# Order of decode steps and late operand loads in a float32 kernel built from seven-product blocks

## The chip, the cores and the metric

The kernel runs on one core of one Trainium2 chip. The metric is the device time of one execution in microseconds (us); before the change its median over 3 runs is 820.87 us (819.47 to 821.22). Details come from one profiled execution, which took 818.6 us itself.

## The reference

A decayed attention recurrence feeds two chains of matrix products. The weights are given as 64-bit numbers and are used as float32.

```python
y[:, :, t] = scale * einsum('bhd,bhde->bhe', q[:, :, t], state)   # 4 x 8 heads, 768 steps, 64 wide
x = y as 3072 x 512
# gated stage, d_ff 1024
a = x @ w1;  b = x @ w2
x = ((a * b) @ w3) @ w_out
# three-matrix stage, d_ff 768
h = maximum(maximum(x @ w1, x @ w2), x @ w3)
out = h @ w_out
```

## The kernel before

The stages follow one another: attention (to about 81 us), the gated stage (L577 to L579, 81.8 to 310.2 us), a merge of `w3` and `w_out` (L665), the product with the merged matrix (L750), the three-matrix stage (L876 to L878, 468.0 to 726.2 us) and the last product (L947).

Every large product is cut into blocks of seven smaller products of sums of quarters, as in Strassen's method. Numbers are split in a high and a low part, so that each piece is three matmuls. In the three-matrix stage there are 3 column groups j, 3 row blocks n in each, and 7 products q in each block: 63 products, numbered s = 7 * (3 * j + n) + q. One product is 3 parts p (one for each weight matrix) of 6 matmuls into one PSUM bank each; two sets of three banks take turns. The gated stage has 2 groups of 3 blocks of 7 products, with 4 parts of 6 matmuls.

After each part the bank is emptied: q = 0 by a ScalarE copy from bank to bank (L881, "seed": set b is then added to by q = 1; in block 0 it goes to SBUF), q = 2 and 3 by ScalarE copies (L883, L885), q = 1 and 6 by a ScalarE copy for part 0 (L891) and a VectorE maximum for the others (L889), q = 4 and 5 by VectorE (L895, then L897). The next product on the same banks can't begin before that.

Beside the products two things are prepared.

*Weights.* A 64-bit weight tile is fetched by a DMA of 512 KB (L93; it is called by a step on the ACT queue, when `late` is set, else on SP) into one of three staging tiles `stg0` to `stg2`, and decoded in steps: ScalarE L124, GpSimd L126, VectorE L147 and L149, ScalarE L156, VectorE L141 (or L135). `decode_a` issues L141 of the tile before, then L124, L147 and L149; `decode_b` issues L156, perhaps the L124 of the next tile, and the next fetch. `Spread` gives the steps out: `Spread(jobs, slots)` releases at its t-th `tick()` so many jobs that after `slots` ticks all are out. The tick stands behind each part.

*Operands.* `make_op` makes an operand by a ScalarE cast (L254) and VectorE subtractions (L255, L266 to L277) in j = 0 and stores it in DRAM; from j = 1 on `op_load` (L724) fetches it back, 1 MB each, on the ACT queue (on SP for the first ones). The buffers form a ring: 4 in j = 0 and j = 2, 6 in j = 1. The load for the next user of a buffer is issued after the last part of the product that frees it (L905 to L907).

Every engine runs its instructions in the order in which they are written, and the DMAs of ScalarE's queue stand in the order of its instructions as well: an instruction that waits holds all that stand behind it.

The lines of the change:

```python
if g or q or not n:                                           # L602
    side.tick()
side = Spread([idle] * 3 + [step] * 36, 4 * (7 * NB - LAG))   # L628
side = Spread([idle] * 2 + [step] * (4 * GH), 2 * 21 + 3)     # L831
t = heir[s]                                                   # L905
if t is not None and not len(GEN) <= t < J1:
    op_load(t)
side.tick()                                                   # L910
```

Of the kernel before, what the change touches and what calls it, by code (L numbers as in the profile page):

```python
# [26 lines left out]
NB = NT // (2 * N)  # L27
# [6 lines left out]
GH = 3  # L34
# [13 lines left out]
def fused_kernel(ctx: ExitStack, tc: tile.TileContext, ck, w12, w3t, wo1, w123, wo2, mask, gout, gch, kdec, out):  # L48
# [16 lines left out]
    def spill(n, q):  # L65
        return opsp[n, q].rearrange("h p x -> p h x")

    def halves(t):
        return t.bitcast(F32).rearrange("p (h x) -> p h x", h=2)
# [349 lines left out]
    def sets_b(blk):  # L419
        s = [bank[0:4], bank[4:8]]  # L420
        return {"a": s[blk % 2], "b": s[1 - blk % 2]}

    with tc.manual_schedule():
# [122 lines left out]
        LAG = 4  # L546
# [6 lines left out]
        side = Spread([idle] * 5 + [step] * (4 * GA), 4 * (12 + LAG))  # L553
        wgen = weights(raw_quads(1024), 1024)
        for g in range(KF // GA):
            for n in range(NB):
                blk = g * NB + n
                sets = sets_b(blk)
                for q in range(7):
                    s = 7 * blk + q  # L560
                    if g == 0:
                        if PB[q] < 0:
                            make_op(s, quad_b, 0)
                        for job in late_w.pop(s, ()):
                            job()
                    t = s + 3
                    if 7 * NB <= t < 14 * NB:
                        nc.scalar.dma_start(out=halves(op_t[t % 4]), in_=spill(t // 7 - NB, t % 7))
                    which, first = ORDER[q]
                    x = op_slot(s)  # L570
                    w = wslot(q).rearrange("p h (i k n) -> p h i k n", i=GA, k=2)
                    seeded = blk in SEED and q == 1
                    for p in range(GA):
                        ps = sets[which][p]
                        for k in range(2):
                            wh, wl = w[:, 0, p, k, :], w[:, 1, p, k, :]
                            nc.tensor.matmul(ps, wh, x[:, 0, k, :], start=first and k == 0 and not seeded, stop=False, skip_group_check=True)  # L577
                            nc.tensor.matmul(ps, wh, x[:, 1, k, :], start=False, stop=False, skip_group_check=True)  # L578
                            nc.tensor.matmul(ps, wl, x[:, 0, k, :], start=False, stop=k == 1, skip_group_check=True)  # L579
                        u, c, e = (part(nm, p) for nm in "UCE")  # L580
                        if q == 0:
                            nc.scalar.copy(out=sets["b"][p] if blk in SEED else u, in_=ps)
                        elif seeded:
                            nc.scalar.copy(out=u, in_=ps)
                        elif q == 1:
                            nc.vector.tensor_tensor(out=u, in0=u, in1=ps, op=ALU.add)
                        elif q == 2:
                            nc.scalar.copy(out=c, in_=ps)
                        elif q == 3:
                            nc.scalar.copy(out=e, in_=ps)  # L590
                        elif q == 4:
                            nc.vector.tensor_tensor(out=e, in0=ps, in1=e, op=ALU.subtract)
                        elif q == 5:
                            nc.vector.tensor_tensor(out=c, in0=c, in1=ps, op=ALU.subtract)
                            nc.vector.tensor_tensor(out=c, in0=c, in1=u, op=ALU.mult)
                            if p % 2:
                                store(fsp[n, p // 2, g], work["C"][:, p // 2 * 1024:][:, :1024], 1)
                        else:
                            nc.vector.tensor_tensor(out=e, in0=e, in1=ps, op=ALU.mult)
                            if p == GA - 1:  # L600
                                store(fsp[n, 6, g], work["E"][:, 1024:], 0)
                        if g or q or not n:  # L602
                            side.tick()
                        if g == 0 and p == PB[q]:
                            make_op(s, quad_b, 0)
                        z = p if blk > NB else 2 * q + p // 2
                        if blk and (q == 0 if blk > NB else q < 2 and p % 2):
                            fsums((blk - 1) % NB, (blk - 1) // NB, z)
                    stores()
                    z = s - 7 * (NB - 1) - LAG  # L610
                    if z == 0:
                        side.rest()
                        drain()
                    if 0 <= z < 7:
                        wgen((0, 4, 1, 2, 3, 5, 6)[z])
                    if z == 6:
                        x_st.close()
                        m_st, m_pl = stage_pool("m")
                        wo1_sb = [m_pl.tile([P, 2, 512], F32R, name=f"wo1_{k}") for k in range(KF)]
                        r_st, r_pl = stage_pool("r", "right")  # L620
                        w3_sb = [(m_pl if k > 1 else r_pl).tile([P, 2, 512], F32R, name=f"w3_{k}") for k in range(10)]
                        w3_sb += [op_t[(k // 2 + 2) % 4][:, :].rearrange("p (u h n) -> p u h n", u=2, h=2)[:, k % 2] for k in range(6)]
                        wq += [lambda k=k: fetch(wo1[k], None, wo1_sb[k][:, 0], wo1_sb[k][:, 1]) for k in range(KF)]
                        wq += [lambda k=k: fetch(w3t[k // 2, k % 2], None, w3_sb[k][:, 0], w3_sb[k][:, 1])
                               for k in range(2 * KF)]
                        wq[-7:-7] = [idle, lambda: ring.__delitem__(slice(3, 5))]
                        more(5)
                        side = Spread([idle] * 3 + [step] * 36, 4 * (7 * NB - LAG))  # L628
        side.rest()

        fraw = [work[nm][:, z * 1024:(z + 1) * 1024] for nm in "UCE" for z in range(2)]
# [42 lines left out]
        side = Spread([step] * 12, 8 * ZD)  # L674
# [42 lines left out]
        J1, J2 = 7 * NB, 14 * NB  # L717
        home_h = [z % 4 for z in range(J1)] + [(4, 5, 1, 2, 3, 0)[z % 6] for z in range(J1)] + [(2, 3, 0, 1)[z % 4] for z in range(J1)]
        bufs_h = [x[:, :] for x in op_t]
        heir = {s: next((t for t in range(s + 1, 7 * NB * GH) if home_h[t] == z), None) for s, z in enumerate(home_h)}  # L720

        def op_load(t):
            eng = nc.sync if t < J1 + 4 else nc.scalar
            eng.dma_start(out=halves(bufs_h[home_h[t]]), in_=spill(t // 7 % NB, t % 7))  # L724
# [3 lines left out]
        side = Spread([idle] * 4 + [step] * (4 * GH), 26)  # L728
        wgen = weights(raw_quads(256 * GH), 256 * GH)
        GEN = (15, 18, 21, 24, 27, 30, 33, 36)  # L730
        XL = 0
        for s in range(XS):
            n, r = divmod(s, 14)
            q, kk = divmod(r, 2)
# [90 lines left out]
        for j in range(GH):  # L825
# [2 lines left out]
                xb_st.close()  # L828
            if j + 1 < GH:
                wq += [lambda w=w, u=u: fetch_w123(j + 1, w, u) for w in range(GH) for u in range(2)]  # L830
                side = Spread([idle] * 2 + [step] * (4 * GH), 2 * 21 + 3)  # L831
            else:
                o_st, o_pl = stage_pool("o")
                wo = [o_pl.tile([P, 2, 768], F32R, name=f"wo{q}") for q in range(7)]
                raw = wraw_t[0][:, :].rearrange("p (m u k n) -> p m u k n", m=2, u=2, k=3)
                wq += [lambda k=k: fetch(wo2[k], raw[:, :, k // 3, k % 3, :]) for k in range(KH)]
                wogen = weights(raw_quads(768), 768, lambda q, n: wo[q])
                side = Spread([idle] * 2 + [step] * (2 * KH) + [drain]
                              + [lambda q=q: wogen(q) for q in (0, 1, 5, 2, 3, 4, 6)], 2 * 21 + 6)
            wgen = weights(raw_quads(256 * GH), 256 * GH)  # L840
            for n in range(NB):
                blk = j * NB + n
                sets = {"a": hbank[blk % 2], "b": hbank[1 - blk % 2]}
                m11, m21, m12, m22 = m_t[blk % 2]
                for q in range(7):
                    s = 7 * blk + q
# [25 lines left out]
                    for p in range(GH):  # L872
# [25 lines left out]
                        if p == GH - 1:  # L898
                            if s == 12:
                                xc_st.close()  # L900
                                xc_st, xc_pl = stage_pool("x2o")
                                bufs_h += [xc_pl.tile([P, 2048], F32R, name=f"opx{z}")[:, :] for z in range(2)]
                            if s in (12, 13):
                                op_load(J1 + s - 12)
                            t = heir[s]  # L905
                            if t is not None and not len(GEN) <= t < J1:
                                op_load(t)  # L907
                        if p == PH[q]:
                            make_op(s, quad_h, len(GEN))
                        side.tick()  # L910
                    if q == 1:
                        store(hsp[n, 0, :, j, :], m11)
                    elif q == 4:
# [18 lines left out]
        for s in range(7 * NB):  # L932
            n, q = divmod(s, 7)
# [99 lines left out]
```

## Time and profile before

| | |
|---|---|
| median of 3 runs | 820.87 us (819.47 to 821.22) |
| profiled execution | 818.6 us, span 816.6 us |
| PE busy | 805.8 us, 99% of the span |
| DVE busy | 631.9 us, 77% |
| ACT busy | 389.1 us, 48% |
| POOL busy | 76.0 us, 9% |
| DMA | 246.56 MB, 302 GB/s |
| granted TensorE clock | 1.00 in the gated and the three-matrix stage |

PE is TensorE's matmuls, PEld its weight loads, one ahead of each matmul; DVE is VectorE, ACT ScalarE (ACTq its queue, where it issues DMAs), POOL GpSimd, SP SyncE. A row of a timeline gives the start, the time it took, engine, line, operation, tiles, and in brackets the idle time ahead of it and who ended that. "DMA to landing" is the time from a DMA's issue to the arrival of its data.

### The profile page before, as it was taken

Reading aid. Unit: us, or ns where it says so; the run is one execution under the profiler, and the core shown is the slowest. Engines: PE = TensorE matmul, PEld = TensorE weight load, DVE = VectorE, ACT = ScalarE, POOL = GpSimd, SP = SyncE. Lnnn points to the kernel's source line nnn. Section 1 sums busy time; section 2 is a strip of 40 time slices with the busy share of each in tenths; the row PEclk is TensorE's granted clock in tenths of the full one; section 3 lists DMA queues with packets and bytes.
Section 4 is the critical chain, followed back from the end, with each engine's and each line's share of the span. In section 5 each row is a group of like instructions: output and inputs, shape, how many; then the busy total and the mean of one; then the engine's idle time right before and its main releaser. Section 6 shows DMA issues by size and latency. Waiting matters only on the chain. (4 is left out here: it accounts for less than half of the span.)

```text
span 816.6 us, 12214 instructions
## 1 busy us (share of the span) xinstructions
PE 805.8 (99%) x4648; PEld 672.5 (82%) x4648; DVE 631.9 (77%) x795; ACT 389.1 (48%) x589; POOL 76.0 (9%) x93
## 2 busy tenths in 40 slices
PE   8999999999999999999999999999999999999997
PEld 8889888888888888888888888888888888888886
DVE  3799899989698978679799848993665555588782
ACT  2432646463345454567577545453334334444642
POOL 2443000000011111001010001000000010000000
PEclk9999999999999999999999999999999999999999
DMA  9998698799999975686789798989998699956522
GB/s 346 407 407 309 226 365 344 274 342 330 388 334 417 352 307 182 241 298 212 269 301 350 275 347 306 369 292 417 394 318 306 239 335 351 326 210 215 193 104 78
DMA packets 70154, 246.56 MB, mean 302 GB/s; under 512 B 6608, under 2 KB 6736, under 8 KB 70096
## 3 DMA queue, kind: packets, MB, share of 16 engines
q1 hardware_dynamic: 48864, 165.97, 53.8%
q10 hardware_dynamic: 21232, 79.81, 27.4%
q8 instruction: 37, 0.61, 0.3%
q14 instruction: 21, 0.17, 0.1%
HBM read 163.97 MB, written 81.79 MB: 301 GB/s over the span
## 5 line engine op out<-in xcount | busy, mean ns | idle before, releaser
L577 PE MATMUL bank<-op,w 128*128 128x512 f32 x336 | 130.8, 389 | 0.0
L579 PE MATMUL bank<-op,w 128*128 128x512 f32 x336 | 130.7, 389 | 0.0
L578 PE MATMUL bank<-op,w 128*128 128x512 f32 x336 | 130.7, 389 | 0.0
L876 PE MATMUL bank<-op,w 128*128 128x512 f32 x330 | 128.6, 390 | 0.1
L878 PE MATMUL bank<-op,w 128*128 128x512 f32 x330 | 128.4, 389 | 0.0
L877 PE MATMUL bank<-op,w 128*128 128x512 f32 x330 | 128.4, 389 | 0.0
L126 POOL TENSOR_SCALAR dec<-dec 128x512 f32<-128x512 f32 x64 | 48.5, 757 | 552.8 <-ACT dec L124 516.1
L577 PEld LDWEIGHTS bank<-op,w 128*128 128x128 f32 x336 | 63.1, 188 | 13.3 <-issue 0.2
L578 PEld LDWEIGHTS bank<-op,w 128*128 128x128 f32 x336 | 63.1, 188 | 13.2
L579 PEld LDWEIGHTS bank<-op,w 128*128 128x128 f32 x336 | 63.1, 188 | 12.9
L876 PEld LDWEIGHTS bank<-op,w 128*128 128x128 f32 x330 | 61.9, 188 | 13.9 <-ACT bank L881 0.9
L878 PEld LDWEIGHTS bank<-op,w 128*128 128x128 f32 x330 | 61.9, 188 | 12.8
L877 PEld LDWEIGHTS bank<-op,w 128*128 128x128 f32 x330 | 61.9, 188 | 12.8
L752 PE MATMUL bank<-op,w 128*128 128x512 f32 x168 | 65.4, 389 | 0.0
L750 PE MATMUL bank<-op,w 128*128 128x512 f32 x168 | 65.4, 389 | 0.0
L751 PE MATMUL bank<-op,w 128*128 128x512 f32 x168 | 65.4, 389 | 0.0
L156 ACT ACTIVATE dec<-stg 128x512 int32<-128x512 uint32 x49 | 33.1, 676 | 52.4 <-DVE stg L149 46.0
L147 DVE TENSOR_SCALAR dec<-dec 128x512 int32<-128x512 int32 x64 | 27.0, 421 | 21.8 <-POOL dec L126 21.8
L124 ACT ACTIVATE dec<-stg 128x512 f32<-128x512 f32 x49 | 32.6, 665 | 13.2 <-DMA stg<-in_w_dram 7.4
L889 DVE TENSOR_TENSOR m<-m,bank 128x512 f32<-128x512 f32 x34 | 23.3, 684 | 19.6 <-PE bank L878 19.0
L948 PE MATMUL bank<-w,wo 128*128 128x512 f32 x96 | 37.4, 390 | 0.0
L947 PE MATMUL bank<-w,wo 128*128 128x512 f32 x96 | 37.4, 389 | 0.0
(216 smaller groups left out, 1581.8 us busy)
## 6 DMA issues: line engine op xcount, KB each, us to landing
op<-opsp ACTq DMA_DIRECT2D x53, 1024.0 KB, 8.1
opsp<-op SPq DMA_DIRECT2D x34, 1024.0 KB, 5.6
ck<-in_ck_dram SPq DMA_DIRECT2D x34, 512.0 KB, 10.0
fsp<-C SPq DMA_DIRECT2D x24, 512.0 KB, 4.8
op<-opsp SPq DMA_DIRECT2D x10, 1024.0 KB, 6.0
hsp<-m SPq DMA_DIRECT2D x32, 256.0 KB, 6.3
stg<-in_w_dram SPq DMA_DIRECT2D x15, 512.0 KB, 9.4
U<-fsp SPq DMA_DIRECT2D x14, 512.0 KB, 5.9
```

Of the source, the lines that this page charges most:

```text
L126: nc.gpsimd.tensor_scalar(out=df, in0=df, scalar1=MAX_HI, scalar2=MIN_HI, op0=ALU.min, op1=ALU.max)
L577: nc.tensor.matmul(ps, wh, x[:, 0, k, :], start=first and k == 0 and not seeded, stop=False, skip_group_check=True)
L578: nc.tensor.matmul(ps, wh, x[:, 1, k, :], start=False, stop=False, skip_group_check=True)
L579: nc.tensor.matmul(ps, wl, x[:, 0, k, :], start=False, stop=k == 1, skip_group_check=True)
L750: nc.tensor.matmul(ps, wh, x[:, 0, k, :], start=first and kk == 0 and k == 0, stop=False, skip_group_check=True)
L751: nc.tensor.matmul(ps, wh, x[:, 1, k, :], start=False, stop=False, skip_group_check=True)
L752: nc.tensor.matmul(ps, wl, x[:, 0, k, :], start=False, stop=kk == 1 and k == 1, skip_group_check=True)
L876: nc.tensor.matmul(ps, wh, x[:, 0, k, :], start=first and k == 0 and not seeded, stop=False, skip_group_check=True)
L877: nc.tensor.matmul(ps, wh, x[:, 1, k, :], start=False, stop=False, skip_group_check=True)
L878: nc.tensor.matmul(ps, wl, x[:, 0, k, :], start=False, stop=k == 1, skip_group_check=True)
L947: nc.tensor.matmul(ps, wh[:, k, o], xh[:, k], start=first and k == 0, stop=False, skip_group_check=True)
L948: nc.tensor.matmul(ps, wh[:, k, o], xl[:, k], start=False, stop=False, skip_group_check=True)
```

## The change

It moves no work between engines and adds or removes no instruction. Three things differ:

1. Gated stage: behind the parts of a block's first product (q = 0) a tick now comes in block 0 of each group only. Before, the second group's blocks had it too. The Spread has 60 slots in place of 68.
2. Three-matrix stage: in the first product of blocks 1 to 8 there is no tick, so no decode step. The Spreads have 39, 36 and 39 slots in place of 45, 45 and 48.
3. Three-matrix stage: the load that belongs to a block's last product (q = 6) is issued after the last seed copy of the next block's first product, together with that product's own load.

```diff
-                        if g or q or not n:
+                        if q or blk in (0, NB):
                             side.tick()
-                        side = Spread([idle] * 3 + [step] * 36, 4 * (7 * NB - LAG))
+                        side = Spread([idle] * 3 + [step] * 36, 60)
-                side = Spread([idle] * 2 + [step] * (4 * GH), 2 * 21 + 3)
+                side = Spread([idle] * 2 + [step] * (4 * GH), (39, 36)[j])
-                              + [lambda q=q: wogen(q) for q in (0, 1, 5, 2, 3, 4, 6)], 2 * 21 + 6)
+                              + [lambda q=q: wogen(q) for q in (0, 1, 5, 2, 3, 4, 6)], 39)
-                            t = heir[s]
-                            if t is not None and not len(GEN) <= t < J1:
-                                op_load(t)
+                            for s0 in {0: (s - 1, s), 6: ()}.get(q, (s,)):
+                                t = heir.get(s0)
+                                if t is not None and not len(GEN) <= t < J1:
+                                    op_load(t)
                         if p == PH[q]:
                             make_op(s, quad_h, len(GEN))
-                        side.tick()
+                        if q or not blk:
+                            side.tick()
```

What it does to the order of the instructions is shown at three places of the three-matrix stage; the numbers behind a tile's name tell the buffer, lines with a minus stand there before, lines with a plus now.

ScalarE, end of block 0 and first product of block 1 (products 4 to 8). `dec` and `stg` are the decode tiles, `op0` and `op1` operands, `E`, `m2048` and the banks belong to the copies behind the parts.

```order
+L156 ACTIVATE dec1_64<-stg0_60 128x512
+L124 ACTIVATE dec0_63<-stg1_61 128x512
 L254 CAST op0_73<-x2_1_3041 128x1024
-L156 ACTIVATE dec1_64<-stg0_60 128x512
-L124 ACTIVATE dec0_63<-stg1_61 128x512
-L93 DMA stg2_62<-in_w123_dram 128x512
 L891 COPY m2048_3813<-bank0_1090 128x512
 L254 CAST op1_1101<-T_1107 128x1024
+L156 ACTIVATE dec0_63<-stg1_61 128x512
+L93 DMA stg2_62<-in_w123_dram 128x512
 L881 COPY bank0_1090<-bank3_1093 128x512
```

The decode of `stg1` now stands ahead of the cast of `op0`, and the fetches of `stg2` and of what follows it come later.

ScalarE, end of block 2 and first product of block 3 (products 20 to 22), where `w6` is a weight cast and `opx0` one of the two further operand buffers.

```order
 L891 COPY m2048_3813<-bank0_1090 128x512
-L724 DMA op0_73<-opsp_74 128x2x1024
 L211 CAST w6_71<-wraw_h_3030 128x768
 L881 COPY bank0_1090<-bank3_1093 128x512
 L881 COPY bank1_1091<-bank4_1094 128x512
 L881 COPY bank2_1092<-bank5_1095 128x512
-L724 DMA opx0_4176<-opsp_74 128x2x1024
+L724 DMA op0_73<-opsp_74 128x2x1024
+L724 DMA opx0_4179<-opsp_74 128x2x1024
```

The load of `op0` moved behind the three seed copies.

ScalarE in block 6 (products 45 and 46), where `stg1` takes a tile of the last weight matrix and `E` the parts of product 45.

```order
+L885 COPY E_1106<-bank5_1095 128x512
+L724 DMA op1_1101<-opsp_74 128x2x1024
 L156 ACTIVATE dec1_64<-stg0_60 128x512
 L93 DMA stg1_61<-in_wo2_dram 128x512
-L885 COPY E_1106<-bank5_1095 128x512
-L724 DMA op1_1101<-opsp_74 128x2x1024
 L124 ACTIVATE dec0_63<-stg1_61 128x512
 L724 DMA op2_1102<-opsp_74 128x2x1024
```

The fetch of `stg1` now stands behind the 1 MB load of `op1`, not ahead of it; the L124 that needs it stands where it stood.

## Rows read from the trace of the kernel before

**Rows 1.** Busy us in a window: span, PE, PEld, DVE, ACT, POOL, clock, DMA

```profile
81.80:310.20 228.40, 228.40 (x1009) 189.11 (x1008) 199.22 (x267) 112.12 (x178) 20.06 (x26) 1.00 0.88 332
```

**Rows 2.** Waits of PEld: in total, how often, the longest

```profile
PEld bank L876 <- ACT bank L881: 1.5, 3, 0.6
```

**Rows 3.** Timeline of PEld: start, duration, instruction; first product and three waits

```profile
468.00 0.19 PEld L876 LDWEIGHTS bank<-op,w 128*128 128x128 f32 x1
...
532.24 0.19 PEld L876 LDWEIGHTS bank<-op,w 128*128 128x128 f32 x1 [0.36 <-ACT bank L881]
...
558.51 0.19 PEld L876 LDWEIGHTS bank<-opx,w 128*128 128x128 f32 x1 [0.54 <-ACT bank L881]
...
673.18 0.19 PEld L876 LDWEIGHTS bank<-op,w 128*128 128x128 f32 x1 [0.56 <-ACT bank L881]
```

**Rows 4.** Timeline of ACT, product 21

```profile
556.71 0.38 ACTq L724 DMA_DIRECT2D op<-opsp  x1
```

**Rows 5.** The fetch of stg1 in product 4, by line 93, and who waited

```profile
L93 SPq DMA_DIRECT2D stg<-in_w_dram x1: 461/461/461, 485.1 to 485.1; - x1
...
  ACT dec L124: 2.6, 1
```

**Rows 6.** Timeline of ACT, products 5 and 6

```profile
488.82 1.06 ACT L254 CAST op<-x 128x1024 fp32r<-128x1024 f32 x1 [3.44 <-PE bank L878]
...
493.11 0.67 ACT L124 ACTIVATE dec<-stg 128x512 f32<-128x512 f32 x1 [2.64 <-DMA stg<-in_w_dram]
```

**Rows 7.** Timeline of DVE, products 5 to 15

```profile
491.15 1.22 DVE L255 TENSOR_TENSOR op<-x,op 128x1024 fp32r<-128x1024 f32 x1
...
494.21 0.68 DVE L895 TENSOR_TENSOR C<-C,bank 128x512 f32<-128x512 f32 x1
...
498.57 0.68 DVE L141 CUSTOM_DVE_ANT_0 wraw_h<-stg,dec 128x1024 uint16<-128x1024 uint16 x1
...
500.24 0.68 DVE L889 TENSOR_TENSOR m<-m,bank 128x512 f32<-128x512 f32 x1
...
512.95 0.42 DVE L147 TENSOR_SCALAR dec<-dec 128x512 int32<-128x512 int32 x1
...
514.74 0.69 DVE L895 TENSOR_TENSOR C<-bank,E 128x512 f32<-128x512 f32 x1 [0.63 <-PE bank L878]
...
530.85 0.68 DVE L889 TENSOR_TENSOR m<-m,bank 128x512 f32<-128x512 f32 x1
```

**Rows 8.** The fetch issued at 508.60, by line 93

```profile
DMA to landing us min/median/max: 4.8/4.8/4.8
```

**Rows 9.** Timeline of ACT, block 6 and start of block 7

```profile
655.41 0.35 ACTq L93 DMA_DIRECT2D stg<-in_wo_dram  x1
...
656.83 0.37 ACTq L724 DMA_DIRECT2D op<-opsp  x1
...
662.36 0.66 ACT L124 ACTIVATE dec<-stg 128x512 f32<-128x512 f32 x1 [5.00 <-DMA op<-opsp]
...
672.56 1.06 ACT L881 COPY bank<-bank 128x512 f32<-128x512 f32 x2
```

**Rows 10.** Timeline of DVE, block 6

```profile
663.75 0.43 DVE L147 TENSOR_SCALAR dec<-dec 128x512 int32<-128x512 int32 x1 [2.17 <-POOL dec L126]
...
664.87 0.68 DVE L895 TENSOR_TENSOR E<-bank,E 128x512 f32<-128x512 f32 x1
...
670.55 0.69 DVE L149 SCALAR_TENSOR_TENSOR stg<-stg,dec 128x512 int32<-128x512 int32 x1
```

**Rows 11.** The fetch issued at 655.41, by line 93

```profile
DMA to landing us min/median/max: 6.9/6.9/6.9
```

**Rows 12.** The load issued at 652.69, by line 724

```profile
DMA to landing us min/median/max: 8.3/8.3/8.3
```

**Rows 13.** The load issued at 656.83, by line 724

```profile
DMA to landing us min/median/max: 7.9/7.9/7.9
```

**Rows 14.** All operand loads of line 724: landing times

```profile
DMA to landing us min/median/max: 4.9/7.7/14.8
```

## Prediction

> **What bounds the kernel now.** I began with the busy time by stretch. In the gated stage TensorE is busy for 228.40 of 228.40 us at a clock of 1.00 [rows 1]: the reader is to see that no other engine can be late there, since TensorE never waits. Next came the waits of PEld, the weight loads that stand ahead of the matmuls. In the three-matrix stage they name one kind, the seed copy L881: 3 times, 1.5 us together, 0.6 the longest [rows 2]. The timeline of PEld places them: 0.36 in product 15, 0.54 at product 22, 0.56 at product 50 [rows 3]. A row of PEld with nothing ahead of it also shows some 0.04 of idle, so the three cost 0.32, 0.50 and 0.52, together 1.34. Everything else in that stage is TensorE at its own pace: (673.18 - 468.00 - 1.34) / 50 = 4.077 us a product [rows 3], 1.36 a part. So the most that the change can give is 1.3 us (0.16%), while the instructions that it moves have due times that they can miss. I take a product's due time as 468.00 + 4.077 s plus the waits before it.
>
> **The change part by part.** It removes and adds nothing; only order changes, so each term is a wait that goes or comes.
>
> *Gated stage: 0.* The steps left out in q = 0 come within the following parts. TensorE's cover is whole [rows 1], since every eviction is ahead of it. If the cover were gone at one place, a VectorE trio of a step (L141, L147, L149) would cost what it takes, 1.67 (498.57 to 500.24 [rows 7]). I take 0.
>
> *Product 22: -0.5.* Before, ScalarE's queue held the load of `op0` until its buffer's store had landed; it went out at 556.71 [rows 4], and the cast of `w6` and the seed copies stood behind it. TensorE got on at 558.51. Now the load stands behind the three copies, and the bank of product 21 is free earlier, so the whole 0.50 goes. What is late next is the load itself, but in j = 1 its ring has six buffers and the operand is due several products later.
>
> *Product 15: the 0.32 stays by itself.* It comes from VectorE: the L889 at 530.85 [rows 7] ends a row of work without a gap since 514.74, and the same instructions stand ahead of it after the change. *Product 50: the 0.52 stays by itself too.* L881 at 672.56 [rows 9] stands behind an L156 and an L124, whose tile VectorE finished with L149 at 670.55 to 671.24 [rows 10]. Both still stand ahead of L881; the load that was moved out from there is an issue in the queue of under 0.4, beside the L124.
>
> *Block 0 to 1: +1.7.* The fetch of `stg1` is issued by SP at 485.1 and an L124 waits for it [rows 5] until 493.11 [rows 6], so it takes 7.9; the change doesn't touch it. Before, the cast of `op0` (488.82) ran ahead of the L124 that waits for this tile (493.11, 2.64 of idle) [rows 6]. Now L156 and L124 stand ahead of the cast, since more steps are released per tick. The cast is held until 493.11 + 0.67, and ends near 494.7. Behind it wait VectorE's L255, before at 491.15, now at 494.7, and in its order the three L895 that empty product 5's banks. From that L255 to the third L895 it was 494.21 - 491.15 = 3.06; now a trio of 1.67 stands between as well: 494.7 + 3.06 + 1.67 = 499.4, and 0.68 for itself, 500.1. Product 7 needs this bank for its third part at 468.00 + 7 x 4.077 + 2.72 = 499.26: a wait of 0.85. The L889 behind it was 6.03 after that L895 (500.24 [rows 7]), with the trio between them; without it 499.4 + 4.36 = 503.8, and with its own 0.69 and a seed copy of 0.57, 505.05. Product 8's third part is due at 503.34 + 0.85 = 504.2: another 0.85. Bounds: 0 (the seed sets and casts take up the delay) to 2.7 (nothing overlaps).
>
> *Block 1 to 2: +1.3.* With no steps in q = 0, the fetch of `stg0` moves to about the place of the fetch issued at 508.60, plus the 1.7 from above: 510.3. With that one's landing time of 4.8 [rows 8] it is there at 515.1. From the start of an L124 to its L147 it takes 1.39 (662.36 [rows 9] to 663.75 [rows 10]), so L147, before at 512.95, comes at 516.5. Of these 3.55, 1.7 is TensorE's own delay, and VectorE had 0.63 idle ahead of the L895 at 514.74 [rows 7]; some 1.25 goes into the row of work that already made product 15 wait. Bounds 0 (the fetch comes earlier) to 1.9 (no idle time takes any of it up).
>
> *Block 6: +3.0.* Here the last weights are decoded. Before, the fetch of `stg1` went out at 655.41 [rows 9] and landed 6.9 later, at 662.3 [rows 11]; L124 waited 5.00 for it and started at 662.36. Now an L885 that waits for TensorE, and the 1 MB load of `op1` (issued 656.83 [rows 9]), stand ahead of the fetch. It can't go out before 657.2, and it follows that load on the same queue. VectorE's L147 (663.75) waits for L124 by way of GpSimd; the L895, L897, L141, L147 and L149 from 664.87 to 670.55 then run without a gap [rows 10], and behind L149 come L156, L124 and the seed copy at 672.56 that product 50 already waits for. So the whole shift of the landing is added at product 50, of which a part shows earlier: the L895 that ended at 665.55 frees the bank that product 48's third part needs at 468.00 + 48 x 4.077 + 2.72 + 0.82 = 667.2, so a shift of over 1.7 shows there already. How large is the shift? With its own 6.9 from 657.2 the fetch lands at 664.1 (+1.8). Put behind `op1` it can't be there before that load, 656.83 + 7.9 = 664.7 [rows 13], and before it came 1.3 after the load ahead of it (652.69 + 8.3 = 661.0 [rows 12]); that gives 666.0 (+3.7). As the load of `op1` no longer has the fetch ahead of it, it may land sooner, so I take 665.3, +3.0. With the shortest landing of a fetch that I have, 4.8 [rows 8], it would be 0.
>
> On this order the Trainium skill, DMA: Bandwidth & Descriptors, section Queues, rings and completion order, says that each DMA engine consumes the descriptors of one issuing queue in ring order, though completions need not come in that order. By this rule a small fetch written behind a 1 MB load starts behind its bytes, which speaks against this change: the term would be +3.0 to +3.7. If the two shared the engines evenly it would be +1.8. The trace agrees as far as it goes: the fetch issued 2.7 after a 1 MB load landed 1.3 after it [rows 11, 12].
>
> *Late loads in j = 2: +0.5.* There the ring has four buffers. A load after product s is for product s + 4 and has three products, 12.2 us. For the loads of products 41, 48 and 55 one product is taken away: 8.2 are left. The landing of these loads takes 4.9 to 14.8, 7.7 in the middle [rows 14]. The first falls in a quiet place, the other two have some tenths each at the middle value, and the last also waits for a seed copy behind a VectorE that has one more weight cast ahead. I take 0.5; bounds 0 and 3.0. In j = 1 the ring of six leaves room.
>
> *Sum.* -0.5 + 1.7 + 1.3 + 3.0 + 0.5 = +6.0, bounds -0.5 and +10.8. The profiled execution takes 818.6 (its span is 816.6), so 824.6 under the profile. The median of the runs shown is 820.87, 0.28% above that execution; I carry the 6.0 over as it is: 826.9.
>
> **The rivals.**
>
> - *Only block 6 pays.* In blocks 0 to 2 the casts and evictions have slack that my chain of VectorE instructions leaves out. For it: those stretches wait for only 0.32 now. Against it: VectorE has no gap from 514.74 to 530.85. -0.5 + 3.0 + 0.5 = +3.0: 823.9.
> - *The fetches come early enough.* Landing times of 4.8 in all three places leave no new wait, and only product 22 gains: -0.5, 820.4. Against it: the fetch of `stg1` in product 4 took 7.9 and its issue doesn't move.
> - *All three seed waits go* (the other side). With no step in a block's first product the copies L881 stand free of L156 and L124. For it: all waits of the stage are on L881. Against it: the order in front of product 50 keeps both. It gives -1.3: 819.5, not slower. It decides from the point at which the steps' tiles are landed before their tick.
> - *The late loads decide.* One load with the longest landing, 14.8, against 8.2 would cost 6.6 beside the rest: 833.5. For it: the DMA queues are filled in j = 2. Against it: the middle is 7.7.
>
> **How the numbers follow.** The forecast has 0.62, only block 6 0.13, early fetches 0.08, all three seed waits 0.10, late loads 0.07. A measurement of this kernel tells about 0.2% (1.6 us) from no change. Faster by more needs more than all waits of the stage seen in the trace, so only half of the third rival could show it: 0.05. Within 0.2%: the other half, the early fetches and a little of the forecast's low end, 0.15. Slower: 0.80. Range: the forecast with its bounds ends at 831.7; I cut it at 831.0 and go down to 820.4, so that the third rival, the late loads and the rims stay out. The forecast's own range is 823 to 831.
>
> **What would show it.** Right: PEld waits at products 7 and 8 near 499 to 505, on banks freed by L895 and L881; a longer wait than 0.4 in product 15; a wait at product 48 and one at product 50, 3.5 together; the fetch of `stg1` in block 6 landing at 664 to 666; no wait at product 22; the gated stage without a wait, as before. Wrong: L124 in block 0 starting well before 493, or the fetch in block 6 landing by 663, or waits on an operand load in products 45, 52 or 59 that are larger than those on banks.

## Result: slower by 0.83%

The changed kernel takes 826.02 us (median of 6 runs, 823.91 to 828.59), the kernel before 819.03 in the runs beside it (6 runs, 817.93 to 821.22). The ratio is 1.0083, 95% interval 1.0059 to 1.0107: 6.8 us more, between 4.8 and 8.8. The forecast was +6.0.

The profiled execution of the changed kernel is the slowest of its six, 828.59 us (span 826.2, against 816.6 before). So it took some 2.6 us more than the median, and terms are better judged by the timed runs of the experiments. First the waits of PEld, as in [rows 2]: what was waited for, us in total, times, longest.

```profile
PEld bank L876 <- ACT bank L881: 3.8, 3, 2.1
PEld bank L876 <- DVE C L895: 2.0, 2, 1.0
PEld bank L876 <- DVE E L895: 1.7, 2, 1.3
PEld bank L876 <- issue: 1.7, 1, 1.7
PEld bank L876 <- DVE m L895: 1.3, 2, 0.9
```

One kind of wait has become five, and three of them name VectorE's L895. The timeline of PEld, as in [rows 3], places the eight that matter; the first product now starts at 470.08.

```profile
499.47 0.19 PEld L876 LDWEIGHTS bank<-op,w 128*128 128x128 f32 x1 [0.86 <-DVE m L895]
...
503.06 0.19 PEld L876 LDWEIGHTS bank<-op,w 128*128 128x128 f32 x1 [0.97 <-DVE C L895]
...
507.91 0.19 PEld L876 LDWEIGHTS bank<-op,w 128*128 128x128 f32 x1 [0.86 <-ACT bank L881]
...
531.52 0.19 PEld L876 LDWEIGHTS bank<-op,w 128*128 128x128 f32 x1 [1.66 <-issue]
...
533.78 0.19 PEld L876 LDWEIGHTS bank<-op,w 128*128 128x128 f32 x1 [1.04 <-DVE C L895]
...
539.95 0.19 PEld L876 LDWEIGHTS bank<-op,w 128*128 128x128 f32 x1 [0.84 <-ACT bank L881]
...
675.72 0.19 PEld L876 LDWEIGHTS bank<-op,w 128*128 128x128 f32 x1 [1.25 <-DVE E L895]
...
683.15 0.19 PEld L876 LDWEIGHTS bank<-op,w 128*128 128x128 f32 x1 [2.09 <-ACT bank L881]
```

The reader is to see three clusters. Products 7 and 8 wait 0.86, 0.97 and 0.86; less 0.04 each that is always there, 2.6. Products 13 to 15 wait 1.66, 1.04, 0.84 and (not shown) 0.44 at 527.25, 3.8 together where 0.32 was. Products 48 and 50 wait 1.25 and 2.09, 3.3 where 0.52 was. The wait at product 22 is gone, and product 62 has a new one of 0.41 (732.46, not shown; what it waits for comes under steps_all). Sum: 2.6 + 3.5 + 2.7 - 0.5 + 0.4 = 8.7; the stage itself grew from 258.14 (468.00 to 726.14) to 266.35 (470.08 to 736.43), by 8.2. Of the rest of the 9.6 by which the span grew, the largest part is two waits in the product with the merged matrix, 0.75 at 358.03 and 0.94 at 361.79.

ScalarE shows the chain of the first cluster and how it goes on into the second (compare [rows 6]; the row of L93 is a fetch's issue).

```profile
495.96 0.66 ACT L124 ACTIVATE dec<-stg 128x512 f32<-128x512 f32 x1 [7.69 <-DMA stg<-in_w_dram]
496.53 1.03 ACT L254 CAST op<-x 128x1024 fp32r<-128x1024 f32 x1
...
502.44 0.66 ACT L156 ACTIVATE dec<-stg 128x512 int32<-128x512 uint32 x1 [3.45 <-DVE stg L149]
502.45 0.33 ACTq L93 DMA_DIRECT2D stg<-in_w_dram  x1
...
513.53 0.33 ACTq L93 DMA_DIRECT2D stg<-in_w_dram  x1
...
519.75 0.66 ACT L124 ACTIVATE dec<-stg 128x512 f32<-128x512 f32 x1 [3.65 <-DMA stg<-in_w_dram]
```

L124 stands ahead of the cast now and holds ScalarE for 7.69 until the fetch lands; before, the cast ran in this gap. VectorE, as in [rows 7] and [rows 10]:

```profile
497.59 1.23 DVE L255 TENSOR_TENSOR op<-x,op 128x1024 fp32r<-128x1024 f32 x1 [4.85 <-ACT op L254]
...
521.14 0.43 DVE L147 TENSOR_SCALAR dec<-dec 128x512 int32<-128x512 int32 x1 [3.67 <-POOL dec L126]
...
673.86 0.43 DVE L147 TENSOR_SCALAR dec<-dec 128x512 int32<-128x512 int32 x1 [5.00 <-POOL dec L126]
```

Each of these idle gaps of VectorE, 4.85, 3.67 and 5.00, stands right ahead of a cluster. L255 waits for the cast that the fetch held; L147 waits twice, by way of GpSimd, for an L124 that a fetch held. While VectorE waits in order, the L895 that free the banks stand behind it. In block 6 ScalarE waits in the same way, as in [rows 9]:

```profile
659.98 0.37 ACTq L724 DMA_DIRECT2D op<-opsp  x1
...
664.54 0.46 ACTq L93 DMA_DIRECT2D stg<-in_wo_dram  x1
672.47 0.66 ACT L124 ACTIVATE dec<-stg 128x512 f32<-128x512 f32 x1 [7.27 <-DMA stg<-in_wo_dram]
```

### The profile page after: what moved, and what is told of

Its sections match the earlier page's. It is cut to its first block, busy times and chain, and to the rows that moved or that the text cites. A ratio compares the mean times of both kernels' runs of the same rounds, so it can differ in the third digit from the quotient of the medians.

```text
span 826.2 us, 12226 instructions
## 1 busy us (share of the span) xinstructions
PE 809.6 (98%) x4648; PEld 672.3 (81%) x4648; DVE 633.8 (77%) x795; ACT 388.8 (47%) x589; POOL 77.9 (9%) x93
## 5 line engine op out<-in xcount | busy, mean ns | idle before, releaser
L126 POOL TENSOR_SCALAR dec<-dec 128x512 f32<-128x512 f32 x64 | 50.4, 787 | 560.8 <-ACT dec L124 461.3
L876 PEld LDWEIGHTS bank<-op,w 128*128 128x128 f32 x330 | 61.9, 188 | 23.3 <-ACT bank L881 3.8
L577 PEld LDWEIGHTS bank<-op,w 128*128 128x128 f32 x336 | 63.1, 188 | 13.5 <-ACT E L590 0.4
L578 PEld LDWEIGHTS bank<-op,w 128*128 128x128 f32 x336 | 63.1, 188 | 13.1
L579 PEld LDWEIGHTS bank<-op,w 128*128 128x128 f32 x336 | 63.1, 188 | 13.1
L878 PEld LDWEIGHTS bank<-op,w 128*128 128x128 f32 x330 | 61.9, 188 | 13.0
L877 PEld LDWEIGHTS bank<-op,w 128*128 128x128 f32 x330 | 62.0, 188 | 12.4
L752 PE MATMUL bank<-op,w 128*128 128x512 f32 x168 | 65.5, 390 | 0.5 <-DVE w L649 0.5
L751 PE MATMUL bank<-op,w 128*128 128x512 f32 x168 | 65.5, 390 | 0.3 <-DVE op L255 0.3
L156 ACT ACTIVATE dec<-stg 128x512 int32<-128x512 uint32 x49 | 33.1, 675 | 54.0 <-DVE stg L149 53.8
L147 DVE TENSOR_SCALAR dec<-dec 128x512 int32<-128x512 int32 x64 | 27.0, 422 | 31.5 <-POOL dec L126 31.5
L124 ACT ACTIVATE dec<-stg 128x512 f32<-128x512 f32 x49 | 32.7, 667 | 29.0 <-DMA stg<-in_w_dram 21.3
L752 PEld LDWEIGHTS bank<-op,w 128*128 128x128 f32 x168 | 31.5, 188 | 7.5 <-DVE w L649 0.9
L751 PEld LDWEIGHTS bank<-op,w 128*128 128x128 f32 x168 | 31.5, 188 | 7.3 <-DVE op L255 0.7
```

The source lines that it names most:

```text
L124: nc.scalar.activation(out=dec.bitcast(F32), in_=top.bitcast(F32), func=ACT.Abs)
L126: nc.gpsimd.tensor_scalar(out=df, in0=df, scalar1=MAX_HI, scalar2=MIN_HI, op0=ALU.min, op1=ALU.max)
L156: nc.scalar.activation(out=dec, in_=low.bitcast(U32), func=ACT.Copy, scale=2.0 ** -29)
L752: nc.tensor.matmul(ps, wl, x[:, 0, k, :], start=False, stop=kk == 1 and k == 1, skip_group_check=True)
```

## The experiments

All were timed in five rounds beside the kernel before. Differences in us are the ratio's distance from 1 times 819; the kernel before had medians of 819.0 to 819.2 there. Most intervals are about 1 us to either side, those of the changed kernel, after_early_fetch and after_fetch_first up to 2, so tenths of a microsecond between two kernels say little.

| kernel | ratio to before (95%) | us |
|---|---|---|
| changed kernel | 1.0083 (1.0059 to 1.0107) | +6.8 |
| gated_only | 1.0006 (0.9993 to 1.0020) | +0.5 |
| loads_only | 0.9979 (0.9970 to 0.9988) | -1.7 |
| steps_j0 | 1.0036 (1.0024 to 1.0049) | +2.9 |
| steps_j1 | 0.9982 (0.9971 to 0.9994) | -1.5 |
| steps_j2 | 1.0025 (1.0012 to 1.0037) | +2.0 |
| steps_all | 1.0072 (1.0060 to 1.0085) | +5.9 |
| no_gated | 1.0087 (1.0075 to 1.0099) | +7.1 |
| after_early_fetch | 1.0056 (1.0037 to 1.0074) | +4.6 |
| after_fetch_first | 1.0053 (1.0037 to 1.0070) | +4.3 |
| after_both | 1.0016 (1.0007 to 1.0026) | +1.3 |
| loads_j1 | 0.9982 (0.9973 to 0.9991) | -1.5 |

### The gated stage's edit

gated_only is the kernel before with this edit; no_gated is the changed kernel without it.

```diff
-                        if g or q or not n:
+                        if q or blk in (0, NB):
-                        side = Spread([idle] * 3 + [step] * 36, 4 * (7 * NB - LAG))
+                        side = Spread([idle] * 3 + [step] * 36, 60)
```

> The kernel before with the gated stage's edit alone (ticks in q = 0 only in block 0 of each group, 60 slots). Theory 1 (from the trace after, where ScalarE and VectorE leave the gated stage some 4.5 us later and the X stage's first two casts come late, 0.75 and 0.94 us of wait): the edit costs 1.5 to 2.5 us, and those two waits at L751 and L752 show again. Rival (my prediction): TensorE's cover in the gated stage hides it and the 1.5 us of the X stage is another execution's scatter: within 0.5 us of before, no wait at L751 or L752.

Measured +0.5, with 0 inside the interval (-0.6 to +1.6), and no wait at L751 or L752. The theory that I formed from the profile after falls as to those two waits, and the prediction's 0 stands within the noise.

> The changed kernel with the gated stage as before (both edits of the three-matrix stage stay). The single edits gave +0.5 us (gated, not told from 0), -1.7 (loads), +2.9 (steps in j = 0) and +2.1 (steps in j = 2); their sum is 3.8, the change itself +6.8. Theory: the edits of the three-matrix stage account for the rest by acting together (and j = 1 gives a little), so this stays at +5.5 to +7 over before. Rival: the late end of the gated stage is what makes the later fetches late, so this comes down to +3.3, the sum without the gated part.

Measured +7.1 where the whole change had +6.8: the gated edit makes no difference inside the change either, and its profile has no wait in the merged product. How much waiting the gated stage and what follows it can show without any edit is seen in steps_j2, where that stage is as before. Its PEld timeline has this row:

```profile
297.69 0.19 PEld L577 LDWEIGHTS bank<-op,w 128*128 128x128 f32 x1 [2.86 <-issue]
```

With 0.98 at 289.53 (not shown) that is 3.8 us of waiting in one execution of unchanged code. The 0.75 and 0.94 at L751 and L752 stand in none of the other four profiles with the gated edit (gated_only, after_early_fetch, after_fetch_first, after_both), so they are scatter of one execution, not the change. A cost of some tenths isn't excluded: all five profiles with the edit have waits in the gated stage itself, 0.35 to 1.5 in all, while five of the eight without it have none, two have 0.15 and 0.33, and steps_j2 has its 3.8.

### The late operand loads

```diff
-                            t = heir[s]
-                            if t is not None and not len(GEN) <= t < J1:
-                                op_load(t)
+                            for s0 in {0: (s - 1, s), 6: ()}.get(q, (s,)):
+                                t = heir.get(s0)
+                                if t is not None and not len(GEN) <= t < J1:
+                                    op_load(t)
```

> The kernel before with the late operand loads' edit alone. Theory: the wait of 0.50 at product 22 goes, those in products 15 and 50 stay, and no load is late in j = 2: -0.5 us, not to be told from no change in the time, but the wait is gone from the weight loads' timeline. Rival (late loads decide): one or more of products 45, 52 and 59 wait for their operand, +0.5 to +3.

Measured -1.7 us, more than expected, and by this the fastest kernel of the study beside loads_j1: 817.69 us, 0.21% under the kernel before. Its waits of PEld in this stage come to one, in product 15:

```profile
PEld bank L876 <- ACT bank L881: 0.4, 1, 0.4
```

Product 22's wait went as predicted, and so did product 50's, which I had said would stay. No product of j = 2 waits.

Product 22's wait is no fixture, though. None of the seven profiles with this edit has it, but of the six without it two, gated_only and steps_all, have none either, and steps_j0 has 0.19. The wait hangs on a store's landing: in gated_only the cast that stands behind the load of `op0` was held by that store as well,

```profile
558.21 0.84 ACT L211 CAST w<-wraw_h 128x768 fp32r<-128x768 f32 x1 [4.41 <-DMA opsp<-op]
```

but the load went out 88.2 us after the start of the stage (557.78, the stage starts at 469.59), against 88.7 before (556.71 and 468.00), and TensorE was not held up.

Why product 50? From product 43 to the last part of product 48 the instructions stand in the same order in before, gated_only, loads_only, loads_j1, steps_j0 and steps_j1, and the wait isn't the same. Landing time of the fetch of `stg1`, from its L93 rows, and product 50's wait:

| kernel | landing, us | idle at product 50, us |
|---|---|---|
| steps_j1 | 5.8 | none |
| loads_only | 6.4 | none |
| loads_j1 | 6.7 | 0.22 |
| before | 6.9 | 0.56 |
| steps_j0 | 7.0 | 0.69 |
| gated_only | 7.7 | 2.05 |

For gated_only, the landing and the wait as the trace has them (first the L93 answer, then PEld's row, then ScalarE ahead of the wait's end):

```profile
DMA to landing us min/median/max: 7.7/7.7/7.7
```

```profile
675.84 0.19 PEld L876 LDWEIGHTS bank<-op,w 128*128 128x128 f32 x1 [2.05 <-ACT bank L881]
```

```profile
674.19 0.67 ACT L124 ACTIVATE dec<-stg 128x512 f32<-128x512 f32 x1 [0.28 <-DMA stg<-in_wo_dram]
...
674.66 0.46 ACTq L724 DMA_DIRECT2D op<-opsp  x1
675.22 0.57 ACT L881 COPY bank<-bank 128x512 f32<-128x512 f32 x1 [0.36 <-ACT dec L124]
```

Six executions put the wait in the order of the landing time; at 6.4 and below there is none. So it follows the fetch, and not the position of L881 alone, and its mean over executions of the kernel before may well be above the 0.52 of the profiled one. The last rows show that the fetch is not all: in gated_only an L124 also waits 0.28 for the fetch that comes after (issued at 667.04, 7.1 to land), and the issue of the 1 MB load, until 675.12, holds L881 for 0.36. The prediction had that issue run beside the L124, as it does in the kernel before; in loads_only it stands behind the copies. How much of the -1.7 comes from this and how much from the landing, and whether the edit shortens the landing or this execution was a lucky one, one trace each can't tell.

### Decode steps, one column group at a time

steps_j0, steps_j1 and steps_j2 are the kernel before with the tick left out in q = 0 and the smaller number of slots in that group alone; here j = 0:

```diff
-                        side.tick()
+                        if q or not blk or j not in (0,):
+                            side.tick()
-                side = Spread([idle] * 2 + [step] * (4 * GH), 2 * 21 + 3)
+                side = Spread([idle] * 2 + [step] * (4 * GH), (39, 45)[j])
```

> The kernel before with the edit on decode steps in column group j = 0 alone (no tick in q = 0 of blocks 1 and 2, 39 slots). Theory: the fetch that ScalarE's L124 waits for now stands ahead of the operand cast, and waits come at products 7, 8 and 13 to 15: +3 by my prediction (1.7 + 1.3), +6 by the trace after (2.6 and 3.8 less the 0.3 that was there). Rival (those waits come from the late start that the gated edit causes): under +1, no wait at products 7 and 8.

Measured +2.9 (2.0 to 4.0; by the medians, 823.18 against 819.12, it is 4.1), near the size that the prediction gave. In its profile product 7 doesn't wait and product 8 only 0.34, since the fetch landed after 6.5 us there (8.7 in the profile after); the second cluster stands in full:

```profile
504.08 0.19 PEld L876 LDWEIGHTS bank<-op,w 128*128 128x128 f32 x1 [0.34 <-ACT bank L881]
...
527.59 0.19 PEld L876 LDWEIGHTS bank<-op,w 128*128 128x128 f32 x1 [1.63 <-issue]
...
529.84 0.19 PEld L876 LDWEIGHTS bank<-op,w 128*128 128x128 f32 x1 [1.04 <-DVE C L895]
...
536.01 0.19 PEld L876 LDWEIGHTS bank<-op,w 128*128 128x128 f32 x1 [0.85 <-ACT bank L881]
```

The rival, that the late start of the stage makes these waits, is out: the stage starts at 468.42 here.

> The kernel before with the edit on decode steps in column group j = 2 alone (no tick in q = 0 of blocks 7 and 8, 39 slots). Theory: the fetch of stg1 in block 6 goes out behind the 1 MB load of op1 and lands 2.5 to 3 us later; waits at products 48 and 50 of 3.0 to 3.5 together where 0.5 was: +2.7. Rival: the shift is given back since product 50 only waits for L881 in any case: under +1.

Measured +2.0 (1.0 to 3.0; by the medians, 822.13 against 819.12, it is 3.0), with the two waits as in the changed kernel:

```profile
672.33 0.19 PEld L876 LDWEIGHTS bank<-op,w 128*128 128x128 f32 x1 [1.45 <-DVE E L895]
...
679.76 0.19 PEld L876 LDWEIGHTS bank<-op,w 128*128 128x128 f32 x1 [2.11 <-ACT bank L881]
```

The fetch of `stg1` went out at 660.92 and took 8.1, so it landed 197.3 after the start of the stage (471.71), against 194.3 before: 3.0 later, the shift that the prediction took.

> The kernel before with the edit on decode steps in column group j = 1 alone (no tick in q = 0 of blocks 4 and 5, 36 slots). Theory: six operand buffers and no operand casts leave room there, no wait at the products 21 to 41 beyond the one at product 22: within 0.5 us of before. Rival: the tighter slots bring waits there too, +1 to +2, which would close the gap between the sum of the single edits and the change.

Measured -1.5, which neither theory had. Products 15 and 22 wait as before (0.34 and 0.42), product 50 doesn't. That is the wait of the table above; why this edit should shorten that landing, far behind it, stays open.

> The kernel before with the late operand loads' edit and the edit on decode steps in j = 1. Alone they gave -1.7 and -1.5 us, though the trace of before has waits of only 1.34 in all in this stage. Theory (both gain by the same waits, those at products 22 and 50, which can go only once): -1.7, as the loads alone. Rival (they gain in different places): -3, about 816.

Measured -1.5: the two gains don't add. What both edits have in common is that product 50 waits little or not at all (0.22 here); product 22's wait, which steps_j1 still has, goes only with the loads' edit, and its half microsecond doesn't show in the times. One wait of 0.32 in product 15 is the only one above 0.3, so there is hardly more to gain; that the gains of 1.5 to 1.7 are larger than the waits seen in the one profile of before isn't explained by any trace.

> The kernel before with the edit on decode steps in all three column groups, the late operand loads as before. The single groups gave +2.9, -1.5 and +2.1, together +3.5; with the loads' edit on top it was +7.1. Theory: groups add up, and the loads' edit is no loss here either, so the difference lies in the steps acting together: +5.5 to +7.5, the waits at products 7 and 8 as large as in the changed kernel. Rival (the loads' edit costs once the steps are bunched): +3 to +4.

Measured +5.9 (4.9 to 7.0), in the theory's range. The groups j = 0 and j = 2 give 5.0 together; the -1.5 of j = 1 is not to be had where the fetch of block 6 is late by order. The waits at products 7 and 8 are there as the theory had them (0.92 and 0.90); a special effect of the steps together isn't needed. With the loads' edit it is 7.1, without 5.9, and the intervals overlap; what that edit costs here, 0 to 2 us, is open. One cost of it shows: the five profiles with both edits have a wait of 0.3 to 1.1 in product 62, which steps_all and steps_j2 don't have. PEld's rows name an L895 for it, but it is the operand that comes last. In no_gated, PE's row and the answer for the load issued at 718.12:

```profile
730.94 0.47 PE L876 MATMUL bank<-op,w 128*128 128x512 f32 x1 [0.68 <-DMA op<-opsp]
```

```profile
DMA to landing us min/median/max: 12.7/12.7/12.7
```

In all five the load lands after 11.9 to 12.7 us and the product starts 0.14 after the landing, while the L895 ended 0.2 to 0.4 ahead of it (in the first cluster TensorE goes on less than 0.1 after an L895); in steps_all it took 10.5 and was there 1.5 ahead. So this is a late operand load, at a product that the prediction's term doesn't name.

### Repairing the two fetches

after_early_fetch is the changed kernel with the third SP fetch of j = 0 issued one product earlier:

```diff
-                    if n == 0 and q in (0, 2, 4):
+                    if n == 0 and q in ((0, 2, 3) if j == 0 else (0, 2, 4)):
```

> The changed kernel with the third of the fetches that SP issues in j = 0 one product earlier (q = 3 in place of q = 4), so that stg1 is there before its L124 stands first. Theory: the wait for this fetch makes the waits at products 7 and 8 (2.6 us in the profile of the changed kernel, less in others), they go; those in products 13 to 15 come from later fetches and stay: 1 to 2.5 us faster than the changed kernel. Rival (the tighter VectorE order itself, with one trio more ahead of the third L895, makes them): no difference, under 0.4.

Measured 1.0056 against 1.0083 to 1.0087: 2.2 to 2.5 us faster than with the late fetch (by the medians, 823.06 against 826.02 and 826.20, some 3; one of its six runs, 827.01, weighs on the ratio). The theory was right on products 7 and 8 and wrong on 13 to 15. All those waits went too; this is the only one left in j = 0, and it was there before the change [rows 3]:

```profile
534.03 0.19 PEld L876 LDWEIGHTS bank<-op,w 128*128 128x128 f32 x1 [0.36 <-ACT bank L881]
```

The ScalarE timeline of this kernel shows why: with L124 done earlier, the next fetch goes out at 491.46, not at 502.45, and the one after that at 498.03, not at 513.53.

```profile
491.45 0.68 ACT L124 ACTIVATE dec<-stg 128x512 f32<-128x512 f32 x1 [3.51 <-DMA stg<-in_w_dram]
491.46 0.33 ACTq L93 DMA_DIRECT2D stg<-in_w_dram  x1
...
498.03 0.33 ACTq L93 DMA_DIRECT2D stg<-in_w_dram  x1
```

The decode is a loop: a fetch may go when a step is through, and a step waits for a fetch. One late fetch makes all that follow late.

after_fetch_first swaps the decode step and the load at one place:

```diff
+                            if s == 45:
+                                side.tick()
                             for s0 in {0: (s - 1, s), 6: ()}.get(q, (s,)):
...
-                        if q or not blk:
+                        if (q or not blk) and (s, p) != (45, GH - 1):
                             side.tick()
```

> The changed kernel with one pair swapped: in block 6, after product 45's last part, the decode step with the fetch of stg1 comes ahead of the 1 MB load of op1, not behind it. The fetch goes out only 0.4 us earlier. Theory (ring order, as in the Trainium skill, DMA: Bandwidth & Descriptors, section Queues, rings and completion order): it lands 1.3 to 2.5 us earlier, and the waits at products 48 and 50 go from 3.3 to 1 to 2; 1.3 to 2.3 us faster than the changed kernel. Rival (the two share the engines evenly): it lands 0.4 earlier, and the time moves by as little.

Measured 1.0053: 2.5 to 2.8 us faster. Issue of the fetch and of the load, and the L124 that waits, in the ScalarE timeline:

```profile
661.18 0.35 ACTq L93 DMA_DIRECT2D stg<-in_wo_dram  x1
661.58 0.45 ACTq L724 DMA_DIRECT2D op<-opsp  x1
...
666.67 0.67 ACT L124 ACTIVATE dec<-stg 128x512 f32<-128x512 f32 x1 [4.35 <-DMA stg<-in_wo_dram]
```

The landing took

```profile
DMA to landing us min/median/max: 5.4/5.4/5.4
```

after the issue, against this in no_gated, which has the same start of the stage to 0.2 us and the fetch behind the load:

```profile
DMA to landing us min/median/max: 8.3/8.3/8.3
```

It went out 0.7 earlier (661.18 against 661.92) and landed 3.6 earlier. By even shares it would have been 0.7; so on this queue the order of writing decides. One pair of executions alone could be scatter, but in all five profiles with the fetch behind the load it took 7.8 to 8.3 (after, no_gated, after_early_fetch, steps_all, steps_j2), and in the two with it ahead 5.2 and 5.4 (after_both, after_fetch_first). The Trainium skill states such an order (DMA: Bandwidth & Descriptors, section Queues, rings and completion order): each DMA engine consumes the descriptors of one queue in ring order. The seven landings agree with it. Product 50's wait is what remained of 2.09:

```profile
677.36 0.19 PEld L876 LDWEIGHTS bank<-op,w 128*128 128x128 f32 x1 [0.33 <-ACT bank L881]
```

> The changed kernel with both repairs: the third SP fetch of j = 0 one product earlier, and the fetch of stg1 in block 6 ahead of the 1 MB load of op1. Each alone took some 2.5 us from the changed kernel's +7, and in their profiles the waits at products 7 to 16 and at 48 and 50 were gone. Theory (these two fetches are the whole loss): what is left is within 0.2% of the kernel before, perhaps 1 us faster as the late loads' edit alone is. Rival (each kept only its own place clean and something else in the new order costs as well, such as the VectorE wait at product 62): +1.5 to +2.5.

Measured 1.0016 (1.0007 to 1.0026), +1.3 us. The two fetches are 5.5 of the 6.8 us. The rest is small and still there, so the rival has a share: in its profile 0.28 of idle is left at product 52 (681.92) and 0.29 at product 62, both for late operand loads. The first has no releaser in the row, but the load of this product's operand, one of those that the change takes a product away from, went out at 674.01 and took 7.8, to 681.82:

```profile
681.92 0.19 PEld L876 LDWEIGHTS bank<-op,w 128*128 128x128 f32 x1 [0.28 <-issue]
```

With both repaired the new order is still 1.3 us slower than the old one, and 3.0 slower than the loads' edit alone, whose gain it ought to hold. What takes these 3 us is open. The profiled execution, 818.71, is 1.7 under the median; against the profile of loads_only it has 0.24 and 0.25 more of waiting at products 52 and 62 and one wait of 0.77 in the gated stage.

## Why the prediction was right, point by point

The forecast was slower by 6.0 us (0.73%), the measured 6.8 (0.83%), in the range and near the forecast.

- *Gated stage, 0*: right within the noise, +0.5 with 0 in the interval, by gated_only and no_gated. The sign that I had set, a gated stage without a wait, did not come: the profile after has 0.35 at 300.05.
- *Product 22, -0.5*: right in place; the wait is gone in every profile with the loads' edit. It is also gone in two without it, so the 0.50 is what one execution had.
- *Product 50's old wait stays by itself*: wrong for the loads' edit alone. I read it as set by the order of L156, L124 and L881. It follows the landing of the fetch, which scatters from 5.8 to 7.7 with the same order, and in gated_only also the load's issue. So loads_only was 1.7 faster, where my terms (-0.5 and +0.5) gave 0.
- *Block 0 to 1, +1.7, and block 1 to 2, +1.3*: +3.0 together, +2.9 by steps_j0. The mechanism of the first is as described: L124 ahead of the cast, then L255, then the third L895 with a trio more; no_gated and steps_all have the two waits that were forecast, 1.7 together. The size hung on luck: I took 7.9 for the landing of the fetch of product 4. In the six kernels that leave j = 0 as it was that of the kernel before is the longest, the others are 5.8 to 6.2; in the five with the new order and this issue it is 6.5 to 8.7, and no run shows why. With 6.5, in steps_j0, the first cluster is 0.3; in the profile after, with 8.7, it is 2.6. The second was under-sized by some 2, 2.9 to 3.5 over before in all five profiles with this order: I let the fetch of `stg0` go at 510.3 and land after 4.8; counted from the stage's start it went 1.2 later in the profile after and took 6.1, because its step stands behind the late fetch before it (L156 waits 3.45 for VectorE). I treated as two terms what is one chain, as after_early_fetch showed.
- *Block 6, +3.0*: right. In steps_j2 the fetch lands 3.0 later. By time it is +2.0 (1.0 to 3.0) in steps_j2 and 2.5 to 2.8 by after_fetch_first. In the profile after L124 starts 194.4 after the stage's start before (662.36 - 468.00) and 202.4 after it now (672.47 - 470.08), 8.0 more. By the load two places ahead of it, issued at 652.69 and now at 659.98, everything there is 5.2 later for other reasons, so the landing is 2.8 later. The due time that I worked out for product 48 still counts the 0.50 of product 22, which by my own term goes; it changes nothing in the sum.
- *Late loads, +0.5*: right in kind and about in size, in another place. In the profile after there is none at products 45, 52 and 59; product 62, which I had not named, waits 0.3 to 1.1 for its load in the five profiles with both edits, and product 52 by 0.24 in after_both.
- *Rivals*: "only block 6 pays" is out by steps_j0; "fetches early enough" happened in part in steps_j0's first cluster and not in the rest; "all three seed waits go" happened in none of the kernels: product 15 kept its 0.3 everywhere; "the late loads decide" is out, as no wait for an operand is above 1.1.

The single edits don't add up to the whole: 0.5 - 1.7 + 2.9 - 1.5 + 2.0 = 2.2, where the whole is 6.8. The two losses alone are 4.9, by the medians 7.1; the gains of the loads' edit and of j = 1 don't show beside them, and product 50 can't lose its wait where the fetch of block 6 is late by order. So the two mechanisms that carry the forecast are the two that carry the loss. That their sizes came so near is in part luck: the first cluster was sized from a landing that five other executions of that order don't repeat, the second was less than half of what the profiles show, and the profiles' waits in j = 0 (3.7 to 6.1) are more than the 2.9 that the timed runs give.

## What to carry to other kernels

A preparation step that is moved out of one stretch gets denser in the next, and a step that waits for a DMA should not come to stand ahead of work that is ready on an in-order engine. When a small transfer that someone will wait for and a large one with slack go to the same queue at about the same time, write the small one first: here this was worth 2.5 us. Of a bundle of edits, time each alone: one of the three was a gain of 0.2%, hidden under a loss of 0.9%.

## What the hardware showed that I had not expected

With the same order of instructions, the same fetch of 512 KB took 5.8 to 7.7 us to land in block 6, and the one of product 4 5.8 to 7.9 in the six kernels that leave j = 0 as it was. What makes it scatter no run here shows. A schedule that just fits one profiled execution has waits of 0 to 2 us at the same place in others, so a wait of half a microsecond in one profile is no safe measure of what removing it gives.
